# A recurrent attention and SiLU kernel: its 1449 steps in a written order with fixed PSUM tiles in place of a list scheduler

## The chip, the cores and the metric

The kernel runs on one core of a Trainium2 chip. The metric is device time of one execution in microseconds (us), measured several times; the profile comes from one more execution, recorded by the hardware profiler. Engines are named as in the profile: PE (TensorE matmuls), PEld (TensorE weight loads), DVE (VectorE), ACT (ScalarE), POOL (GpSimd), SP (SyncE, which here only issues transfers).

## The reference

Two blocks follow each other. The first is a recurrence over 768 tokens for 4 batches and 8 heads, with a state of 40 x 40 for each head; its output is the input of a dense block with a SiLU gate, 3072 tokens by 320 channels, 2048 hidden channels.

```
for t in range(S):
    y[:, :, t] = np.einsum('bhd,bhde->bhe', rt, state)
    Sa = np.einsum('bhde,bhe->bhd', state, at)
    state_decay = state * wt[:, :, None, :] - np.einsum('bhd,bhe->bhde', Sa, bt)
    state = state_decay + np.einsum('bhd,bhe->bhde', vt, kt)
x = y, as (4 * 768) rows of 8 * 40
h = x @ w_in
out = (h / (1 + exp(-h))) @ w_out
```

All inputs are float32 except `w_in` and `w_out`, which are float64.

## The kernel before

The sequence is cut into 12 chunks of 64 tokens. Within a chunk the recurrence is written as small matrix products, with a triangular system of 64 x 64 for each of 32 pairs of batch and head that has to be inverted. The code is a list of steps, each a Python function that issues a handful of instructions on one engine:

- `load(n)` and `load_r(n)` bring a chunk's inputs in (SP transfers of 512 KB, 96 KB and 160 KB).
- `prepare(n)` scales them on DVE (`down`, `between_` and `up` with the two scans of L627 and L645, the products of L654 and L664) and multiplies on PE (`between`, L682; `turn`, L769; `sv`, L744). The first product goes by way of DRAM (`ms<-sb`, L699).
- `special(n)`, for chunks 0 to 2, inverts the triangular systems: `xs<-ms` (L871) brings 16 x 16 blocks, DVE inverts them in a chain of short products and sums (`dots`, L795 and L796), `zs` and `mi` (L881, L887) carry them back, and PE and DVE then take turns three times (`more`, L958 on PE, the addition L973 on DVE). Before that DVE masks the block matrix `sb` (L900).
- `inverse(k)` and `merge(n)` do the same from chunk 3 on, for two chunks at once: a longer chain of L795 and L796 on DVE, transfers `zd`, `ZQ`, `xd` and `X`, then `merge` on PE (L1039, copies on ACT and DVE, L1068).
- `chain(n)` carries the state (PE L1111, L1135, L1166, L1196, L1223), `read(n)` makes the output of the recurrence (PE L1269, L1308, L1323; DVE masks of L1281 and the product of L1334).
- `moe(n)` is the dense block for 256 tokens: `full` (L1405) and `rest` (L1418), the gate on ACT (L1428), then `second` (L1445) and a copy to `ot` (L1457). One `full` is 8 matmuls of 128 x 128 by 256 columns, one `second` 4 of 128 x 128 by 320. The profile counts each float32 matmul as two instructions, so there a `full` is x16 and a `second` x8; the rows of the instruction order below count it once.
- `weights(n)`, ten units of 1 MB, fetches float64 weights with POOL transfers (L479) and puts them together as float32: DVE L484, L486, L487 and L493 or L500, ACT L485, L488 and L502, and for the first three units sums on PE (`sum_`, L508) with a product on DVE (L520).

PSUM is cut into four tiles of two banks each, called `pair`; two more tiles, `lam`, lie in SBUF. A step that needs one of them holds a `Room`, and the room gets its tile from whoever orders the steps.

What sets the order: each step says what it reads and writes, so that `Plan.add` knows which steps have to come before it. `Plan.order` is a list scheduler: it keeps an estimated clock for each engine, transfers and instruction fetches among the estimates, and takes the step that could start first, with a priority by chunk. `Plan.best(10, 400)` calls it 410 times when the kernel is built, with other weights and other priorities, values each order with the estimates of `Plan.through` and keeps the best. The steps are then issued in that order. Each engine works off its own instructions strictly in the order in which they were issued; SP, ACT and POOL also issue transfers, each its own queue in order. So the order that the scheduler writes is what each engine and queue follows, and an instruction that waits holds all those behind it on its engine.

```
    with tc.manual_schedule():
        for op in plan.best(10, 400):
            op["do"]()
```

Of the kernel before, what the change touches and what calls it, by code (L numbers as in the profile page):

```python
# [33 lines left out]
class Plan:  # L34
# [4 lines left out]
    def __init__(self, slots):  # L39
        self.slots = slots  # L40
        self.free = {k: [(0.0, i) for i in range(len(v))] for k, v in slots.items()}
        self.ops, self.wrote, self.read = [], {}, {}
# [23 lines left out]
    HOP = {"SP": 0.1, "ACT": 0.15, "PE": 0.15, "DVE": 0.15, "POOL": 0.2}  # L66
    RATE, LAND = 300.0, 2.0
    COLD = 42.0
    URGE = {"SP": 0.0, "ACT": 0.03, "PE": 0.05, "DVE": 0.1, "POOL": 0.02}
    LEAVE = {"F": 0.09, "R": 0.2, "T": 0.13, "Q": 0.13, "H": 0.12, "S": 0.11}  # L70
    ENTER = {"F": 0.08, "R": 0.1, "T": 0.03, "Q": 0.03, "H": 0.03, "S": 0.03}

    def turn(self, op):

        a, b = self.shape, op["shape"]
        if a == b or {a, b} == {"R", "T"}:
            return 0.03 if a != "F" else 0.0
        return self.LEAVE[a] + self.ENTER[b]

    def walk(self, start, cost, k, keep=False):  # L80


        fetched, count, t = self.fetched[-2:], self.count, start
        step, end = cost / max(k, 1) * (2 if start < self.COLD else 1), count + k
        have = len(self.fetched)
        while count < end:
            block = count // 256
            gate = 256 * block + 194
            if have == block + 1:
                fetched.append(max(t + 0.4, fetched[-1] + 2.6) + 1.3)  # L90
                have += 1
            if count >= gate:
                t = max(t, fetched[-1] + 0.1)
            to = min(end, gate if count < gate else 256 * block + 256)
            t += (to - count) * step
            count = to
        if keep:
            self.fetched += fetched[2:]
            self.count = end
        return t  # L100

    def order(self):
        ops = self.ops
        self.fetched, self.count, self.shape = [0.0, 0.0], 0, "Q"
        nexts = [[] for _ in ops]
        for op in ops:
            op["wait"] = len(op["before"])
            for b in op["before"]:
                nexts[b].append(op)
        ready = {e: [op for op in ops if op["engine"] == e and not op["wait"]] for e in self.HOP}  # L110
        at = dict.fromkeys(self.HOP, 0.0)
        out, held = [], {}
        queue = dict.fromkeys(("SP", "ACT", "POOL"), 0.0)
        for op in ops:
            op["ready"] = 0.0
        while len(out) < len(ops):
            best = None
            for e, some in ready.items():
                starts = []
                for op in some:  # L120
                    s = max(at[e], op["ready"])
                    for room in op["rooms"]:
                        if room.slot is None:
                            free = self.free[room.kind]
                            fits = free and held.get((room.kind, room.most), 0) < room.most
                            s = max(s, min(free)[0]) if fits else 1e9
                    lost = 0.0
                    if e == "PE" and s < 1e8:
                        lost = self.walk(s + self.turn(op), op["cost"], op["k"]) - s - op["cost"]
                    starts.append((s, s + lost, op))  # L130
                if not starts:
                    continue
                urge = self.URGE[e]
                s, _, op = min(starts, key=lambda x: (x[1] + urge * x[2]["pri"], x[2]["n"]))
                if best is None or s < best[0]:
                    best = s, op
            s, op = best
            assert s < 1e8, "no room"
            e = op["engine"]
            ready[e].remove(op)  # L140
            if e == "PE":
                at[e] = end = self.walk(s + self.turn(op), op["cost"], op["k"], True)
                self.shape = op["shape"]
            else:
                at[e] = end = s + op["cost"]
            if op["size"]:
                begin, work = max(queue[e], end), op["size"] / self.RATE
                both = max(0.0, max(queue[o] for o in queue if o != e) - begin)
                queue[e] = begin + (2 * work if work < both / 2 else work + both / 2)
                for o in queue:  # L150
                    if o != e and queue[o] > begin:
                        queue[o] += min(work, both / 2)
                end = queue[e] + self.LAND
            op["start"], op["end"] = s, end
            for room in op["rooms"]:
                if room.slot is None:
                    room.slot = self.free[room.kind].pop(self.free[room.kind].index(min(self.free[room.kind])))[1]
                    room.end = 0.0
                    held[room.kind, room.most] = held.get((room.kind, room.most), 0) + 1
                room.left -= 1  # L160
                room.end = max(room.end, end)
                if not room.left:
                    held[room.kind, room.most] -= 1
                    self.free[room.kind].append((room.end + 0.1, room.slot))
            for x in nexts[op["n"]]:
                x["ready"] = max(x["ready"], end + (self.HOP[x["engine"]] if x["engine"] != e else 0.0))
                x["wait"] -= 1
                if not x["wait"]:
                    ready[x["engine"]].append(x)
            out.append(op)  # L170
        return out

    SLOW = 2.8, 1.7
    CASES = (1.0, 300.0, 0.15, 1.0), (1.5, 240.0, 0.15, 1.0), (1.5, 240.0, 0.25, 1.04)
    WINDOW, FEW = 3.41, 0.42

    def through(self, out, crowd, rate, hop, slower):

        at = dict.fromkeys(self.HOP, 0.0)
        queue = dict.fromkeys(("SP", "ACT", "POOL"), 0.0)
        end, free = [0.0] * len(out), {}
        fetched, count, shape, work = [0.0, 0.0], 0, "Q", {}
        before, after = self.SLOW
        width, few = self.WINDOW, self.FEW
        for op in out:
            e = op["engine"]
            s = at[e]
            for b in op["before"]:  # L190
                s = max(s, end[b] + (hop if self.ops[b]["engine"] != e else 0.0))
            for place in op["takes"]:
# [39 lines left out]
    def best(self, draws, steps):  # L232

        rng = Random(1)
# [1425 lines left out]
```

## Time and profile before

| | us |
|---|---|
| median of 3 runs | 733.7 |
| lowest and highest | 732.0, 738.74 |
| span of the profiled execution | 734.2 |
| PE busy | 676.8 |
| PE idle before its first matmul | 13.7 |
| PE idle from 21 us on, up to 36.2 | 15.1 |
| last matmul ends, span ends | 726.2, 734.2 |
| DVE busy | 419.7 |
| ACT busy | 194.1 |

The page gives busy time for each engine, the granted TensorE clock in slices (PEclk), the load of the 16 DMA engines, the chain of work that ended last, and groups of equal instructions. Finer views of the same execution list instructions in order of time, with the idle time before them and what ended it, or give the busy time of every engine in chosen stretches. In such rows the first number is the start, the second the length, and "x64" the number of instructions. "issue" as the releaser means that the engine waited for nothing that the profile shows.

### The profile page before, as it was taken

The numbers are of one execution on the slowest core, as the hardware profiler recorded it, in microseconds if no ns is written. First come the engines' busy times: TensorE is split into PE (matmuls) and PEld (weight loads), VectorE is DVE, ScalarE is ACT, GpSimd is POOL, SyncE is SP. The second block draws the span as 40 slices with busy tenths as digits, with TensorE's granted clock in tenths as the row PEclk, the third lists the DMA queues.
The fourth block names the chain that finished last, engine by engine and source line by source line (L and its number), as shares of the span: only waits on it lengthen the run. The fifth ranks groups of instructions, "written<-read, shape, count | busy, mean of one in ns | idle before, by whom it ended". The sixth has DMA issues, their size and how long they took to land.

```text
span 734.2 us, 27298 instructions
## 1 busy us (share of the span) xinstructions
PE 676.8 (92%) x12666; PEld 542.3 (74%) x12666; DVE 419.7 (57%) x614; ACT 194.1 (26%) x241; POOL 15.2 (2%) x35
## 2 busy tenths in 40 slices
PE   2179899998999999999999999999999999999995
PEld 2177568787778678878778878778777778787773
DVE  6845799977469348397364883372992676020000
ACT  3251625422302413304312305132104312102020
POOL 2101000000000000000000000000000000000000
PEclk9996999999899999999999999999997999999998
DMA  7680754751721554417355306354215033201001
GB/s 249 150 235 27 205 194 128 223 128 37 177 93 25 137 138 141 126 46 162 81 136 142 103 19 145 87 149 130 66 27 119 26 103 108 44 20 41 18 1 22
DMA packets 117921, 77.15 MB, mean 105 GB/s; under 512 B 65538, under 2 KB 114229, under 8 KB 117160
## 3 DMA queue, kind: packets, MB, share of 16 engines
q1 hardware_dynamic: 113220, 64.43, 33.5%
q0 software_dynamic: 2224, 10.63, 4.4%
q8 instruction: 101, 1.65, 0.9%
q10 hardware_dynamic: 2356, 0.26, 0.3%
q14 instruction: 20, 0.16, 0.1%
HBM read 60.29 MB, written 14.61 MB: 102 GB/s over the span
## 4 chain that ended last, share of the span: by engine, by line
PE 86%; DVE 5%; ACT 3%; issue 2%; DMA 1%; SPq 1%; ACTq 0%; DVEq 0%
PE pair L1445 30%; PE pair L1405 23%; PE pair L1418 6%; PE pair L1269 4%; PE pair L682 3%; PE pair L1323 3%; PE pair L958 2%; PE pair L1223 2%; PE pair L744 2%; PE pair L1135 2%; PE pair L1068 2%; PE pair L1308 1%; PE pair L1111 1%; PE pair L1166 1%; PE pair L508 1%
## 5 line engine op out<-in xcount | busy, mean ns | idle before, releaser
L1445 PE MATMUL pair<-wo,gts 128*128 128x320 f32 x768 | 221.6, 445 | 0.2 <-issue 0.2
L1445 PEld LDWEIGHTS pair<-wo,gts 128*128 128x128 f32 x768 | 145.7, 193 | 60.5 <-issue 4.3
L1405 PE MATMUL pair<-xt,wi 128*128 128x256 f32 x768 | 176.6, 387 | 0.2 <-DVE wi L520 0.2
L1405 PEld LDWEIGHTS pair<-xt,wi 128*128 128x128 f32 x768 | 145.6, 192 | 22.8 <-issue 1.3
L1428 ACT ACTIVATE gts<-pair 128x1024 f32<-128x1024 f32 x48 | 46.5, 1020 | 107.5 <-PE pair L1418 100.4
L1457 DVE COPY ot<-pair 128x320 f32<-128x320 f32 x24 | 11.8, 491 | 95.2 <-PE pair L1445 93.5
L682 PE MATMUL pair<-a,kb 40*64 40x64 f32 x1536 | 33.5, 241 | 33.5 <-DVE a L654 28.7
L796 DVE TENSOR_REDUCE XI<-XI 128x64 f32<-128x512 f32 (+9 forms) x85 | 58.7, 690 | 2.9
L682 PEld LDWEIGHTS pair<-a,kb 40*64 40x64 f32 x1536 | 29.7, 153 | 36.6 <-issue 18.4
L1418 PE MATMUL pair<-xt,wi 64*128 64x256 f32 x384 | 47.9, 389 | 0.0
L1418 PEld LDWEIGHTS pair<-xt,wi 64*128 64x128 f32 x384 | 35.1, 187 | 6.3 <-issue 2.0
L1334 DVE TENSOR_TENSOR lam<-pair,wz 128x1024 f32<-128x1024 f32 x11 | 13.5, 1224 | 41.6 <-PE pair L1323 41.4
L1281 DVE TENSOR_TENSOR lam<-pair,ml 128x1024 f32<-128x1024 f32 x22 | 26.5, 1220 | 14.0 <-PE pair L1269 12.4
L795 DVE TENSOR_TENSOR XI<-XI,mi 128x1024 f32<-128x1024 f32 (+8 forms) x60 | 33.7, 561 | 1.5
L1269 PEld LDWEIGHTS pair<-r,vut 40*64 40x64 f32 x1536 | 26.3, 142 | 6.4 <-issue 4.8
L1269 PE MATMUL pair<-r,vut 40*64 40x64 f32 x1536 | 29.3, 228 | 1.1 <-issue 1.1
L664 DVE TENSOR_TENSOR kb<-kbv 128x512 f32<-128x512 f32 (+1 forms) x36 | 29.8, 860 | 0.2
L1001 ACT COPY mi<-XI 128x1024 f32<-128x1024 f32 x5 | 10.1, 2023 | 70.6 <-DVE XI L796 70.6
L627 DVE TENSOR_TENSOR_SCAN kbv<-wz,zt 128x1024 f32<-128x1024 f32 x12 | 27.5, 2292 | 0.5
L645 DVE TENSOR_TENSOR_SCAN wz<-wz,zt 128x1024 f32<-128x1024 f32 x12 | 27.5, 2291 | 0.4
L795 DVE TENSOR_TENSOR XI<-XI,xs 128x1024 f32<-128x1024 f32 (+1 forms) x25 | 25.2, 1009 | 0.7
L407 ACT ACTIVATE vu<-pair 64x640 f32<-64x640 f32 x13 | 9.1, 700 | 58.8 <-PE pair L1135 56.0
(152 smaller groups left out, 686.8 us busy)
## 6 DMA issues: line engine op xcount, KB each, us to landing
wz<-in_wT SPq DMA_DIRECT2D x12, 512.0 KB
kbv<-in_bT SPq DMA_DIRECT2D x12, 512.0 KB
a<-in_aT SPq DMA_DIRECT2D x12, 512.0 KB
kbv<-in_kT SPq DMA_DIRECT2D x12, 512.0 KB
r<-in_rT SPq DMA_DIRECT2D x48, 96.0 KB
vut<-in_vT SPq DMA_DIRECT2D x48, 96.0 KB
vu<-in_v SPq DMA_DIRECT2D x24, 160.0 KB
out<-ot SPq DMA_DIRECT2D x48, 80.0 KB
```

Of the source, the lines that this page charges most:

```text
L627: nc.vector.tensor_tensor_scan(back(V), back(W[:, 2 : 2 + Q * C]), zt, 1.0, ALU.mult, ALU.add)
L645: nc.vector.tensor_tensor_scan(Z, Z, zt, 0.0, ALU.mult, ALU.add)
L664: TTn[engine].tensor_tensor(out=at_(kb, place(is_b, first), (576 * step, 4 // step), (128, 4), (1, C)), in0=blocks((kf, bf)[is_b]), in1=bl ...
L682: nc.tensor.matmul(room.tile[half(b), j, g * C : g * C + C], lhsT=kb[rows(j), place(is_b, q) : place(is_b, q) + C], rhs=A[rows(j), q * C : ...
L795: nc.vector.tensor_tensor(out=at_(tmp, 0, *dims), in0=x, in1=y, op=ALU.mult)
L796: nc.vector.tensor_reduce(out=out_, in_=at_(tmp, 0, *dims), axis=AX.X, op=ALU.add)
L1269: nc.tensor.matmul(pl.tile[half(1 - b if role else b), b, c * C : c * C + C], lhsT=vut[rows(b), role, hu, :], rhs=rs[rows(b), hh, :], star ...
L1281: lambda pl=pl, la=la: nc.vector.tensor_tensor(out=la.tile.rearrange("p (q t) -> p q t", q=Q), in0=pl.tile.rearrange("p a b -> p (a b)").r ...
L1405: nc.tensor.matmul(rooms[g].tile[:, f // 2, (f % 2) * T : (f % 2) * T + T], lhsT=wi[:, k, (4 * g + f) * 128 : (4 * g + f) * 128 + 128], rh ...
L1418: nc.tensor.matmul(rooms[g].tile[:, h, (f % 2) * T : (f % 2) * T + T], lhsT=wi3[half(h), g * 256 + (f % 2) * 128 : g * 256 + (f % 2) * 128 ...
L1428: nc.scalar.activation(out=gts[:, 4 * g * T : 4 * g * T + 4 * T], in_=rooms[g].tile.rearrange("p a b -> p (a b)"), func=AF.Silu)
L1445: nc.tensor.matmul(po[b].tile[:, 0, 0:DM], lhsT=g4[:, f, 128 * b : 128 * b + 128], rhs=wo[:, f, :], start=f == 0, stop=f == NF - 1,)
```

## The change

The scheduler, its estimates and its search are taken out. In their place stands `Plan.follow`, which takes two tables written into the file: `ORDER`, the numbers of all 1449 steps in the order in which they are issued, and `SLOTS`, one digit for each room, the tile that it gets. The steps themselves, what each reads and writes, and every instruction and transfer that a step issues are the same as before: 383 steps on PE, 391 on DVE, 223 on ACT, 21 on POOL and 431 on SP. Only their order within each engine and queue changes, and which of the four `pair` tiles (or two `lam` tiles) a step uses. Lines after L262 move up by 144 (L958 becomes L814).

```diff
-    def order(self):
...
-    def through(self, out, crowd, rate, hop, slower):
...
-    def best(self, draws, steps):
...
+    def follow(self, order, slots):
+
         rooms = {id(room): room for op in self.ops for room in op["rooms"]}
+        assert sorted(order) == list(range(len(self.ops))) and len(slots) == len(rooms)
+        for room, slot in zip(rooms.values(), slots):
+            room.slot, room.tile = int(slot), self.slots[room.kind][int(slot)]
+        done = set()
+        for n in order:
+            assert self.ops[n]["before"] <= done
+            done.add(n)
+        return [self.ops[n] for n in order]
+
+ORDER = """
+0 3 2 1 84 86 5 7 6 8 116 12 9 10 11 13 15 14 117 90 31 16 29 22 20 23 17 91 25 24 19 21 18 92 118 30 94 33 85
...
+SLOTS = """
+03002133122302302010321213033023202300211303211223101103300221000023321202000110213203100101302001012022313320
...
     with tc.manual_schedule():
-        for op in plan.best(10, 400):
+        for op in plan.follow([int(n) for n in ORDER.split()], "".join(SLOTS.split())):
             op["do"]()
```

In the rows below the tile names carry the numbers of their buffers (`sb_90` is the block matrix of chunk 1, `sb_89` that of chunks 0 and 2; `pair_111` to `pair_114` are the four PSUM tiles).

The first place is the stretch in which chunk 0's inverse ends and chunk 1's begins, about 35 to 56 us, on SP and on DVE. SP before, the last of eight loads of `r` and `vut` and what follows them:

```order
L592 DMA r<-in_rT 48x2x256
L601 DMA vut<-in_vT 48x2x256
L575 DMA vu_100<-in_v 64x2x320 x2
L699 DMA ms<-sb_90 16x16x16 x8
L871 DMA xs<-ms 128x256
```

SP now, from the transfers `mi` of chunk 0's inverse on:

```order
L743 DMA mi<-zs 16x16x16 x4
L457 DMA vut<-in_vT 48x2x256
L555 DMA ms<-sb_90 16x16x16 x8
L727 DMA xs<-ms 128x256
L457 DMA vut<-in_vT 48x2x256
L448 DMA r<-in_rT 48x2x256
```

The eight pieces of `ms` and the `xs` behind them now come ahead of all but one of the loads of `r`, `vut` and `vu_100`. On POOL, which issued three 1 MB fetches of weights in a row here (one into `raw`, two into `wo`), the second fetch into `wo` now stands behind a transfer of `read(0)`'s result. DVE before, at the additions of `special(0)`, from the third to what follows the last:

```order
L973 TENSOR_TENSOR XI<-pair_112,X_94 128x4x128
L973 TENSOR_TENSOR XI<-pair_113,X_94 128x4x128
L973 TENSOR_TENSOR X_94<-pair_114,X_94 128x4x128
L973 TENSOR_TENSOR X_94<-pair_111,X_94 128x4x128
L900 TENSOR_TENSOR sb_90<-sb_90,ml 128x1024
L729 TENSOR_TENSOR lam_116<-pair_113,ml 128x1024
```

DVE now, from the first of these additions to the fifth:

```order
L829 TENSOR_TENSOR XI<-pair_113,X_94 128x4x128
L343 TENSOR_SCALAR gts<-gts 128x1024
L340 TENSOR_SCALAR wi<-wo 128x2x512
L829 TENSOR_TENSOR XI<-pair_114,X_94 128x4x128
L756 TENSOR_TENSOR sb_90<-sb_90,ml 128x1024
L829 TENSOR_TENSOR XI<-pair_111,X_94 128x4x128
L829 TENSOR_TENSOR XI<-pair_113,X_94 128x4x128
L340 TENSOR_SCALAR wi<-raw_137 128x2x512
L829 TENSOR_TENSOR X_94<-pair_114,X_94 128x4x128
```

Between the additions (L829) there now stand steps of the weights and the mask of `sb_90`, which came later before. A little earlier on DVE, `down`, `between_` and `up` of chunk 1 and its product into `a_84` now stand ahead of the chain of short products and sums of `special(0)`; before, `between_`, `up` and that product stood behind it.

The second place is PE at the third inverse, `special(2)`. Before, from its first product to the next `full`:

```order
L682 MATMUL pair_111<-a_83,kb 64x64 x32
L958 MATMUL pair_113<-XI 64x64 x32
L744 MATMUL pair_114<-vu_100,lam_115 64x40 x32
L958 MATMUL pair_111<-XI 64x64 x32
L769 MATMUL pair_113<-ident,kb 128x40 x16
L1405 MATMUL pair_114<-xt,wi 128x256 x8
```

Now:

```order
L1261 MATMUL pair_114<-xt,wi 128x256 x8
L538 MATMUL pair_111<-a_84,kb 64x64 x32
L814 MATMUL pair_112<-XI 64x64 x32
L1261 MATMUL pair_113<-xt,wi 128x256 x8
L814 MATMUL pair_111<-XI 64x64 x32
L1274 MATMUL pair_114<-xt,wi_67 128x256 x4
```

Long matmuls of `moe(1)` (L1261, L1274) now stand between the products of `special(2)`.

The third is PE at `merge(9)`. Before:

```order
L1405 MATMUL pair_112<-xt,wi 128x256 x8
L682 MATMUL pair_111<-a_85,kb 64x64 x32
L769 MATMUL pair_113<-ident,kb 128x40 x16
L1039 MATMUL pair_111<-ZQ,sb_90 32x32 x32
L769 MATMUL pair_113<-ident,kb 128x40 x16
L682 MATMUL pair_111<-a_85,kb 64x64 x32
L1068 MATMUL pair_113<-X_95,ZQ 32x32 x32
L1405 MATMUL pair_111<-xt,wi 128x256 x8
```

Now:

```order
L895 MATMUL pair_113<-ZQ,sb_90 32x32 x32
L1274 MATMUL pair_112<-xt,wi_67 128x256 x4
L1274 MATMUL pair_114<-xt,wi_67 128x256 x4
L1052 MATMUL pair_111<-ident,G 104x40 x16
L538 MATMUL pair_113<-a_85,kb 64x64 x32
L600 MATMUL pair_112<-vu_99,lam_116 64x40 x32
L924 MATMUL pair_114<-X_95,ZQ 32x32 x32
L1261 MATMUL pair_113<-xt,wi 128x256 x8
```

The two matmul steps of `merge(9)` (L1039 and L1068 before, L895 and L924 now) have other work between them than before, and on DVE the whole of `inverse(3)`, which ends ahead of them, now stands in front of the preparation of chunk 11 and no longer behind it.

More of the change, by code (lines that the diff above doesn't have):

```diff
@@ L3 @@
 from math import prod
-from random import Random
 import concourse.bass as bass
@@ L40, in __init__ @@
         self.slots = slots
-        self.free = {k: [(0.0, i) for i in range(len(v))] for k, v in slots.items()}
         self.ops, self.wrote, self.read = [], {}, {}
@@ L64, in add @@
         return op
[L66 to L100, printed above, removed]
@@ L102, in order @@
-    def order(self):
[L103 to L171, printed above, removed]
@@ L173 @@
-    SLOW = 2.8, 1.7
-    CASES = (1.0, 300.0, 0.15, 1.0), (1.5, 240.0, 0.15, 1.0), (1.5, 240.0, 0.25, 1.04)
-    WINDOW, FEW = 3.41, 0.42
-    def through(self, out, crowd, rate, hop, slower):
[L181 to L192, printed above, removed]
-                s = max(s, free.get(place, 0.0))
-            if e == "PE":
-                self.shape = shape
-                t, shape = s + self.turn(op), op["shape"]
-                to_ = count + op["k"]
-                step = op["cost"] / op["k"]
-                while count < to_:
-                    block = count // 256
-                    gate = 256 * block + 194
-                    if len(fetched) == block + 1:
-                        full = crowd if max(queue.values()) > t + 1 else 0.0
-                        fetched.append(max(t + 0.4, fetched[-1] + before) + after + full)
-                    if count >= gate:
-                        t = max(t, fetched[-1] + 0.1)
-                    to = min(to_, gate if count < gate else 256 * block + 256)
-                    left, count = (to - count) * step, to
-                    while left > 1e-9:
-                        w = int(t / width)
-                        pace = 0.5 if t > 30 and work.get(w - 1, 0.0) < few * width else 1.0
-                        d = min((w + 1) * width - t + 1e-9, left / pace)
-                        work[w] = work.get(w, 0.0) + d
-                        t += d
-                        left -= d * pace
-            else:
-                t = s + op["cost"] * (slower if e == "DVE" else 1.0)
-            at[e] = t
-            if op["size"]:
-                begin, work_ = max(queue[e], t), op["size"] / rate
-                both = max(0.0, max(queue[o] for o in queue if o != e) - begin)
-                queue[e] = begin + (2 * work_ if work_ < both / 2 else work_ + both / 2)
-                for o in queue:
-                    if o != e and queue[o] > begin:
-                        queue[o] += min(work_, both / 2)
-                t = queue[e] + self.LAND
-            end[op["n"]] = t
-            for place in op["gives"]:
-                free[place] = max(free.get(place, 0.0), t + 0.1)
-        return max(end)
```

55 lines of the change are left out of this document (4 added, 51 removed), and 56 rows, old and new, of the table ORDER.

## The prediction

> **What bounds the kernel now.** I read the page first, then the stretches of busy time, then the rows of PE in order of time, with what ended each idle time.
>
> ```profile
> PE 676.8 (92%) x12666; PEld 542.3 (74%) x12666; DVE 419.7 (57%) x614; ACT 194.1 (26%) x241; POOL 15.2 (2%) x35
> PE 86%; DVE 5%; ACT 3%; issue 2%; DMA 1%; SPq 1%; ACTq 0%; DVEq 0%
> 100.00:150.00 50.00, 47.28 (x843) 37.35 (x838) 45.86 (x65) 24.23 (x27) 1.59 (x3) 0.97 0.67 210
> 650.00:700.00 50.00, 50.00 (x527) 39.70 (x526) 5.06 (x6) 5.96 (x8) 0.00 (x0) 1.00 0.10 27
> ```
>
> PE is 86% of the chain that ended last, and from 650 to 700 us it is busy without a gap. The change removes no matmul, so it can only give back time in which PE stands still or runs slowly. PE stands still for 734.2 - 676.8 = 57.4 us. Of these the next rows fix the parts that an order can hardly touch:
>
> ```profile
> 13.66 3.69 PE L682 MATMUL pair<-a,kb 40*64 40x64 f32 x128 [13.66 <-DVE a L654]
> 36.16 1.99 PE L682 MATMUL pair<-a,kb 40*64 40x64 f32 x64 [15.07 <-DVE a L654]
> 726.85 1.11 SPq L1460 DMA_DIRECT2D out<-ot  x2
> ```
>
> 13.7 us before the first product, 15.1 us while DVE inverts chunk 0's blocks, and 8.0 us from the last matmul's end at 726.2 on, 0.6 for the copy and 7.4 for the last transfer. That leaves 57.4 - 13.7 - 15.1 - 8.0 = 20.6 us of PE gaps, spread from 46 to 560 us. The second loss is slow running. In the stretches the last three numbers are the granted clock, the DMA share and GB/s:
>
> ```profile
> 42.00:46.00 4.00, 3.49 (x94) 3.25 (x91) 1.38 (x2) 4.00 (x6) 0.00 (x0) 1.00 1.04 319
> 46.00:50.00 4.00, 3.25 (x106) 3.21 (x109) 2.07 (x3) 0.50 (x1) 0.00 (x0) 1.00 1.06 283
> 58.00:62.00 4.00, 4.00 (x104) 2.74 (x106) 0.61 (x1) 0.07 (x1) 0.00 (x0) 0.50 0.02 4
> 66.00:70.00 4.00, 4.00 (x121) 3.07 (x118) 1.77 (x6) 1.03 (x2) 0.00 (x0) 0.89 0.02 4
> 196.00:200.00 4.00, 3.85 (x129) 3.16 (x122) 2.05 (x2) 0.00 (x0) 0.00 (x0) 0.57 0.57 115
> 248.00:252.00 4.00, 4.00 (x70) 2.51 (x68) 0.00 (x0) 0.79 (x2) 0.00 (x0) 0.60 0.68 149
> 560.00:564.00 4.00, 4.00 (x118) 3.73 (x111) 0.18 (x1) 1.60 (x2) 0.00 (x0) 0.50 0.56 92
> ```
>
> Four times the clock falls to half: from about 53 to 67 us, around 196 to 203, 247 to 252 and 557 to 568. Each time PE had just stood still.
>
> **The first patch, 36 to 100 us.** Two waits for nothing but the next instruction come just after 8 us in which the DMA engines were full (share 1.04 and 1.06):
>
> ```profile
> 46.75 3.31 PE L958 MATMUL pair<-XI 64*64 64x64 f32 x102 [1.26 <-issue]
> 53.32 0.34 PE L1166 MATMUL pair<-X,R 64*40 64x64 f32 x3 [2.76 <-issue]
> 59.27 3.69 PE L1269 MATMUL pair<-r,vut 40*64 40x64 f32 x128
> 289.81 2.09 PE L1269 MATMUL pair<-r,vut 40*64 40x64 f32 x128
> 35.86 1.42 POOL L479 DMA_DIRECT2D wo<-in_w_in  x2
> wo<-in_w_in POOLq DMA_DIRECT2D x2, 1024.0 KB, 13.2
> 41.48 11.30 SPq L699 DMA_DIRECT2D ms<-sb  x8
> 54.42 1.23 DVE L900 TENSOR_TENSOR sb<-sb,ml 128x1024 f32<-128x1024 f32 x1 [3.62 <-DMA ms<-sb]
> ```
>
> The waits are 4.0 us. Behind them the half clock costs, from 53.3 to about 67 us (0.89 in the window 66 to 70 is 0.9 us of it): 14 us of PE work at 3.69 against 2.09 us for the same 128 matmuls, 14 x (1 - 2.09 / 3.69) = 6.1 us. Together 10 us. The load is three fetches of 1 MB (two of them 13.2 us on the way), eight loads of `r` and `vut` and two of `vu`, and behind all these eight small pieces of `ms` that took 11.3 us to issue. The change takes one 1 MB fetch out of this stretch and puts `ms` ahead of seven of the eight loads. At 300 GB/s, near the rates of the two full stretches, 1 MB is 3.5 us less to carry before the next instructions come. I take 6 of the 10 us: the wait of 2.76 us goes below the point at which the clock falls, the other stays. Bounds: all 10 (the matmul work at 45 us finds free DMA engines), or nothing (the loads are only shifted by a few us).
>
> [...]
>
> On DVE `special(1)` moves forward, and weights are put together in gaps in which DVE waited for PE:
>
> ```profile
> 43.72 0.69 DVE L973 TENSOR_TENSOR XI<-pair,X 128x512 f32<-128x512 f32 x1 [4.01 <-PE pair L958]
> 92.38 1.22 DVE L973 TENSOR_TENSOR XI<-pair,X 128x1024 f32<-128x1024 f32 x1
> 90.22 2.08 PE L958 MATMUL pair<-X,XI 64*64 64x64 f32 x64 [1.25 <-ACT X L405]
> 109.94 1.10 PE L1166 MATMUL pair<-X,R 64*40 64x64 f32 x64 [1.62 <-ACT gts L1428]
> ```
>
> The row at 92.38 is `special(1)`'s first addition. Its blocks come by way of `ms`, whose pieces ended 54 us in, so it can start earlier by what `ms` gains; from 100 to 150 us DVE is busy 45.86 of 50, so work done in the gaps before helps there. Of the PE gaps from 74 to 110 us (these two and five shorter ones, some 5 us) I take 3. Chunk 1's preparation also loses the scan of 2.3 us and more from the way between `special(0)`'s chain and its first product at 36.16, but gets two masks of 1.23 us and a weights step in return, and the first product of all comes a product later: 1 us, no more. Start in all: -10 us, bounds 0 and -18. What hides the moved weights steps is DVE's wait of 4.01 us; if the 1 MB for `wo` lands later than the additions need, DVE stands at that step (`wi<-wo`) and holds them up (first rival).
>
> **The second patch, 160 to 204 us.** Before, 992 matmuls in small products run with hardly a long one between them, and PE waits for instructions again:
>
> ```profile
> 167.99 0.63 PE L682 MATMUL pair<-a,kb 40*64 40x64 f32 x27 [0.86 <-issue]
> 171.81 0.61 PE L744 MATMUL pair<-vu,lam 64*64 64x40 f32 x28 [0.81 <-issue]
> 195.79 1.25 PE L682 MATMUL pair<-a,kb 40*64 40x64 f32 x60 [0.92 <-issue]
> 199.79 14.69 PE L1445 MATMUL pair<-wo,gts 128*128 128x320 f32 x47 [0.15 <-issue]
> 523.70 17.49 PE L1445 MATMUL pair<-wo,gts 128*128 128x320 f32 x64
> ```
>
> Gaps of 0.86 + 0.81 + 0.92 and 0.4 us for one more, 3.0 us. Then 47 matmuls take 14.69 us where 47 / 64 x 17.49 = 12.8 would do, 1.9 us more, and the small products ahead of them, at 0.57 in the window 196 to 200, some 1 us more: 3 us of half clock. Now `full`, `rest` and the first `second` of `moe(1)` stand between the products. I take 5 of the 6 us; bounds 0 and 6.
>
> **The merges at 246 and 557 us.** The four small steps around `merge(9)` wait for each other:
>
> ```profile
> 547.97 1.22 DVE L796 TENSOR_REDUCE XI<-XI 128x128 f32<-128x1024 f32 x1
> 246.31 0.69 PE L769 MATMUL pair<-ident,kb 40*128 40x40 f32 x16 [0.81 <-DVE ZQ L409]
> 557.15 0.75 PE L1039 MATMUL pair<-ZQ,sb 32*32 32x32 f32 x64 [0.72 <-DVE lam L729]
> 559.34 1.99 PE L682 MATMUL pair<-a,kb 40*64 40x64 f32 x64 [0.81 <-DVE ZQ L409]
> 563.10 6.44 PE L1405 MATMUL pair<-xt,wi 128*128 128x256 f32 x16
> 550.99 3.72 PE L1405 MATMUL pair<-xt,wi 128*128 128x256 f32 x16
> ```
>
> 1.5 us of waits, then 6.44 - 3.72 = 2.7 us lost on one `full` and by the same ratio 1.6 on the two small steps before it: 5.8 us. Now `inverse(3)` stands ahead of chunk 11's preparation on DVE (two scans and four products, some 10 us), and the two halves of the merge have `rest`, L1052, L538 and L600 between them. The merge near 246 has a wait of 0.8 us and a patch of 4 us at 0.60, which is 3.2 us at half clock and 1.4 lost: 2.2 us. I take 7 of the 8.0; bounds 0 and 8.0.
>
> **What comes in.** The other waits of PE for instructions (six short ones, some 3 us in all) stay, since the small steps between long ones are as many as before:
>
> ```profile
> 353.10 0.62 PE L682 MATMUL pair<-a,kb 40*64 40x64 f32 x26 [0.83 <-issue]
> ```
>
> Two runs of small products grow to 672 matmuls, at chunks 5 and 7; a run of about that length cost this 0.83 us and no patch. The tables were fixed for one set of moments and the chip has its own: I add 3 us, bounds 0 and 7 (one more patch like that at 557, 5.8).
>
> **Sum.** -10 - 5 - 7 + 3 = -19: the profiled 734.2 goes to 715. The median 733.7 lies 0.5 under the profiled span, so the forecast for the runs is 715. Ends: 733.7 - (18 + 6 + 8) = 702, 733.7 + 7 = 741. A measurement of this kernel tells about 1% from no change, 7.3 us: faster means under 726.4, slower over 741.
>
> **Rivals.** First, the start gains nothing. If the first fetch into `wo` again takes 13.2 us from 35.2, it lands at 48.4; three additions, the mask and a second weights step then follow, some 6 us, and `special(0)` ends at 55 where it ended at 50.8. That eats the 6 us of the clock patch, and the three us on DVE stay in doubt: start 0, sum 733.7 - 9 = 725, with 720 to 735 around it. For it speaks that DVE works in order; against it that only 2 MB are under way, not 3.
>
> Second, the start gains more. If DVE runs without gaps from 50 us on, the additions of `special(1)` come some 10 us before 92.38, and `moe(1)`, which begins at 150.5, comes 15 to 17 us sooner. With the other terms (-5, -7, +3) that is a sum of -25 or so, 708, and down to 702 with less coming in. Against it speaks that PE and DVE take turns in it.
>
> ```profile
> 150.51 7.07 PE L1405 MATMUL pair<-xt,wi 128*128 128x256 f32 x32
> ```
>
> Third, slower: half clock patches where none is now. Each costs 4 to 10 us with its gap (the four above). The order is tight everywhere, and a transfer that comes 2 us late in a run of small products is enough, as at 53 us. To be slower than 741 the kernel must have about as much lost in patches as now, and two new ones of 5 us on top: from the sixth on. For it speaks that runs of 672 matmuls appear; against it that 300 to 550 us had only short waits and no patch at runs as long.
>
> That the change does nothing is excluded: the order differs on every engine.
>
> **Chances.** The forecast (710 to 724) 0.58, start gains nothing 0.19 (a third of it still under 726.4), start gains more 0.14, slower patches 0.09. Faster 0.58 + 0.14 + 0.06 = 0.78, same 0.13, slower 0.09. The range leaves out one in ten above and one below: 702 to 731.
>
> **What would show it.** In the profile after: no `issue` wait over 2 us and no clock under 0.9 between 50 and 66 us; the addition of `special(1)` before 86 us; the first `full` of `moe(1)` 8 to 12 us before 150; no patch at the place of `special(2)` or of `merge(9)`. A DVE wait over 3 us at the weights step between the additions of `special(0)` would show the first rival, five or more clock patches the third.

## The result, and the profile after

| | before | after |
|---|---|---|
| median, us | 733.25 (4 runs, 732.0 to 738.74) | 703.77 (4 runs, 702.16 to 707.02) |
| span of the profiled execution, us | 734.2 | 700.4 |
| PE busy, us | 676.8 | 654.6 |

The ratio of the runs is 0.9569, with a 95% interval of 0.9511 to 0.9626: 29.5 us, where the forecast had 19. The profiled executions differ by 33.8 us.

From the profile's page, the busy time of each engine and the engines' shares of the chain that ended last:

```profile
PE 654.6 (93%) x12666; PEld 532.4 (76%) x12666; DVE 417.6 (60%) x614; ACT 193.9 (28%) x241; POOL 18.1 (3%) x35
PE 88%; DMA 5%; DVE 2%; SPq 1%; issue 1%; ACT 1%; POOL 0%; DVEq 0%; POOLq 0%
q8 instruction: 101, 1.65, 1.0%
```

The same 12,666 matmuls keep PE busy for 22.2 us less, so most of the gain isn't idle time but cheaper work. The third line is the queue that carries instructions; it will matter below. The stretches (start and end, length, then PE, weight loads, DVE, ACT and POOL busy, the granted clock, DMA share, GB/s):

```profile
36.00:60.00 24.00, 18.77 (x428) 15.39 (x422) 13.90 (x31) 10.79 (x15) 1.91 (x3) 0.93 0.50 142
60.00:100.00 40.00, 35.81 (x838) 27.16 (x832) 33.21 (x36) 17.29 (x21) 5.48 (x8) 0.96 0.65 178
150.00:200.00 50.00, 49.94 (x1200) 41.77 (x1199) 38.70 (x59) 16.31 (x22) 1.12 (x2) 1.00 0.38 102
200.00:250.00 50.00, 50.00 (x981) 40.77 (x982) 30.88 (x38) 14.00 (x18) 0.00 (x0) 1.00 0.45 119
500.00:550.00 50.00, 50.00 (x979) 41.33 (x978) 28.31 (x47) 13.88 (x17) 0.00 (x0) 1.00 0.45 115
```

From 110 us to the last matmul the clock never falls, and PE has one wait of 0.47 us. The rows that answer to those of the prediction (start, length, and in brackets the wait before and its releaser):

```profile
45.77 0.69 DVE L340 TENSOR_SCALAR wi<-wo 128x1024 int32<-128x1024 int32 x1
50.31 1.23 DVE L756 TENSOR_TENSOR sb<-sb,ml 128x1024 f32<-128x1024 f32 x1 [3.25 <-DMA ms<-sb]
52.19 3.39 PE L814 MATMUL pair<-XI 64*64 64x64 f32 x64 [3.06 <-DVE XI L829]
83.27 1.23 DVE L829 TENSOR_TENSOR XI<-pair,X 128x1024 f32<-128x1024 f32 x1 [0.51 <-PE pair L814]
87.04 3.27 PE L1261 MATMUL pair<-xt,wi 128*128 128x256 f32 x7 [3.35 <-DMA vut<-in_vT]
106.08 3.72 PE L1261 MATMUL pair<-xt,wi 128*128 128x256 f32 x16 [1.18 <-ACT gts L1284]
142.18 3.62 PE L1261 MATMUL pair<-xt,wi 128*128 128x256 f32 x16
521.25 0.75 PE L895 MATMUL pair<-ZQ,sb 32*32 32x32 f32 x64
521.93 2.00 PE L1274 MATMUL pair<-xt,wi 64*128 64x256 f32 x16
526.26 1.20 PE L924 MATMUL pair<-X,ZQ 32*32 32x32 f32 x64
```

`special(1)`'s first addition comes at 83.27 (92.38 before), `moe(1)` begins at 142.18 (150.51 before), and `merge(9)` runs without a wait. The start has three new waits of its own: 3.25 us of DVE for `ms`, 3.06 and 3.35 us of PE.

**Where the 33.8 us lie.** To compare stretches in which the steps stand in another order, I gave each kind of matmul a price: what it takes from its start to the next one's where PE doesn't wait, from 150 us on (the 30% quantile over the profiles; about 15 ns in L538, 222 in L1261, 275 in L1301). Time that has passed, less the prices of all matmuls started, is what was lost until then:

| stretch, us | lost before | lost after | difference |
|---|---|---|---|
| 0 to 140 | 58.2 | 52.2 | -6.0 |
| 140 to 200 | 7.4 | 1.5 | -5.9 |
| 200 to 240 | 2.1 | 0.2 | -1.9 |
| 240 to 260 | 4.0 | 0.1 | -3.9 |
| 260 to 540 | 10.6 | 3.0 | -7.6 |
| 540 to 580 | 7.0 | 0.3 | -6.7 |
| 580 to the tail | 1.9 | 0.1 | -1.8 |

From 140 us on the old order lost 10.5 us in waits (5.9 with "issue" as the releaser, 4.0 on DVE, 0.7 on ACT), 7.8 at half clock, and 14.8 in matmuls that took longer than their price at full clock. After, these are 0.5, 0 and 4.5. What slows the matmuls of the last group was not tried by itself.

### The profile page after: what moved, and what is told of

It reads as the page before. It is cut to its first block, busy times and chain, and to the rows that moved or that the text cites. A ratio compares the mean times of both kernels' runs of the same rounds, so it can differ in the third digit from the quotient of the medians.

```text
span 700.4 us, 27219 instructions
## 1 busy us (share of the span) xinstructions
PE 654.6 (93%) x12666; PEld 532.4 (76%) x12666; DVE 417.6 (60%) x614; ACT 193.9 (28%) x241; POOL 18.1 (3%) x35
## 3 DMA queue, kind: packets, MB, share of 16 engines
q8 instruction: 101, 1.65, 1.0%
## 4 chain that ended last, share of the span: by engine, by line
PE 88%; DMA 5%; DVE 2%; SPq 1%; issue 1%; ACT 1%; POOL 0%; DVEq 0%; POOLq 0%
PE pair L1301 30%; PE pair L1261 25%; PE pair L1274 7%; PE pair L538 4%; PE pair L1125 4%; PE pair L1179 3%; PE pair L1079 2%; PE pair L814 2%; PE pair L625 2%; PE pair L1022 2%; PE pair L1164 1%; PE pair L600 1%; PE pair L924 1%; PE pair L991 1%; PE pair L967 1%; DMA ms<-sb 1%
## 5 line engine op out<-in xcount | busy, mean ns | idle before, releaser
L1301 PE MATMUL pair<-wo,gts 128*128 128x320 f32 x768 | 216.7, 437 | 0.0
L1301 PEld LDWEIGHTS pair<-wo,gts 128*128 128x128 f32 x768 | 143.3, 190 | 57.2 <-issue 0.7
L1261 PE MATMUL pair<-xt,wi 128*128 128x256 f32 x768 | 176.1, 385 | 4.5 <-DMA vut<-in_vT 3.4
L1261 PEld LDWEIGHTS pair<-xt,wi 128*128 128x128 f32 x768 | 145.0, 191 | 26.9 <-issue 3.8
L1274 PE MATMUL pair<-xt,wi 64*128 64x256 f32 x384 | 47.9, 389 | 0.0
L538 PE MATMUL pair<-a,kb 40*64 40x64 f32 x1536 | 30.5, 232 | 15.1 <-ACT kbv L531 14.5
L538 PEld LDWEIGHTS pair<-a,kb 40*64 40x64 f32 x1536 | 27.1, 145 | 21.6 <-ACT kbv L531 14.5
L1274 PEld LDWEIGHTS pair<-xt,wi 64*128 64x128 f32 x384 | 35.2, 187 | 4.9 <-issue 0.7
L638 ACT COPY kt<-pair 128x640 f32<-128x640 f32 x24 | 16.6, 692 | 49.5 <-PE pair L625 49.5
L1125 PEld LDWEIGHTS pair<-r,vut 40*64 40x64 f32 x1536 | 24.2, 135 | 3.2 <-issue 2.2
L1125 PE MATMUL pair<-r,vut 40*64 40x64 f32 x1536 | 26.3, 220 | 0.0
L600 PE MATMUL pair<-vu,lam 64*64 64x40 f32 x768 | 14.6, 232 | 12.5 <-DVE lam L585 12.0
```

What stands on the lines that cost most here:

```text
L538: nc.tensor.matmul(room.tile[half(b), j, g * C : g * C + C], lhsT=kb[rows(j), place(is_b, q) : place(is_b, q) + C], rhs=A[rows(j), q * C : ...
L1125: nc.tensor.matmul(pl.tile[half(1 - b if role else b), b, c * C : c * C + C], lhsT=vut[rows(b), role, hu, :], rhs=rs[rows(b), hh, :], star ...
L1261: nc.tensor.matmul(rooms[g].tile[:, f // 2, (f % 2) * T : (f % 2) * T + T], lhsT=wi[:, k, (4 * g + f) * 128 : (4 * g + f) * 128 + 128], rh ...
L1274: nc.tensor.matmul(rooms[g].tile[:, h, (f % 2) * T : (f % 2) * T + T], lhsT=wi3[half(h), g * 256 + (f % 2) * 128 : g * 256 + (f % 2) * 128 ...
L1301: nc.tensor.matmul(po[b].tile[:, 0, 0:DM], lhsT=g4[:, f, 128 * b : 128 * b + 128], rhs=wo[:, f, :], start=f == 0, stop=f == NF - 1,)
```

## Experiments

The first nine keep every step as it is and change `ORDER` or `SLOTS` alone; the last six do one small step more than once, with the same result. Ratios are to the kernel before on the same chip; its medians there were 734.5 to 738.6 us, so ratios, not times, are compared with the 0.957 of the change. The cuts of code give each edit in short: `OLD` and `NEW` stand for the orders before and after, `OLD_SLOTS` for the tiles before, and the kernels hold the finished tables. Where two orders are joined or steps of the new one are moved on PE, 8 to 89 of the 312 tiles also differ from the change's (`slots`).

**Which part of the order?** The two orders joined at the first product of `moe(1)`, in two runs:

```diff
-for op in plan.follow(ORDER, SLOTS):
+for op in plan.follow(NEW[:375] + [n for n in OLD if n not in NEW[:375]], slots):
```

> The changed kernel's first 375 steps (up to the first product of the dense block for chunk 1, 142 us in its profile), then the 1074 others in the order in which the kernel before has them. Theory (the gain lies after 150 us, where waits of PE for instructions and half-clock patches are gone): the start alone brings what that first product came earlier, 8 us, so 733.3 - 8 = 725 us, with the half-clock patch and the waits near 165 to 200 us back. Rival (a better start lets everything behind it follow without waits): near the changed kernel, 700 to 708 us.

741.66 us (10 runs), ratio 1.008 (1.004 to 1.012): 0.8% slower than before, where the theory had 725 us. Part of it is a wait of 8.15 us where the changed kernel, with the same order up to there, had 3.35, so transfers at the start vary by some us from run to run. Behind the joint the old waits are back:

```profile
93.53 6.12 PE L1261 MATMUL pair<-xt,wi 128*128 128x256 f32 x16 [8.15 <-DMA xt<-X]
168.71 0.44 PE L538 MATMUL pair<-a,kb 40*64 40x64 f32 x11 [0.76 <-issue]
```

```diff
+for op in plan.follow(OLD[:395] + [n for n in NEW if n not in OLD[:395]], slots):
```

> The kernel before's first 395 steps (up to the same product, 150 us in its profile), then the others in the changed kernel's order. Theory: all of the steady part's gain without the start's, 733.3 - 22 = 711 us (708 to 714). Rival (the start carries the gain): 725 to 733 us. A third case, that the two halves fit badly where they are joined, would show as waits of PE at 140 to 170 us.

708.14 us, ratio 0.963 (0.955 to 0.970). The order behind `moe(1)`'s first product makes nearly all of the gain; the new start adds some 4 us by the medians, which is not clear of the noise, and nothing when the old order follows it.

```diff
+for op in plan.follow(NEW[:375] + sorted(NEW[375:690], key=OLD.index) + NEW[690:], slots):
```

> The changed kernel with one stretch in the kernel before's relative order: its steps 375 to 690, about 142 to 240 us, in which chunk 2's inverse is finished and ten small PE steps then stand in a row. Theory: that train of small steps brings back the PE waits of 0.4 to 0.9 us for instructions and the half-clock patch seen there before, some 5 us of waits and 2 us of clock, so 703.8 + 7 = 711 us. Rival (the order inside that stretch is no cause, the gain is spread over later stages): 702 to 706 us.

728.06 us, ratio 0.989 (0.982 to 0.997), much more than the theory's 711. The old waits are back up to 300 us, and where the stretch joins the new order PE waits 4.67 us more for a mask:

```profile
315.78 1.95 PE L1164 MATMUL pair<-r,GT 40*40 40x64 f32 x64 [4.67 <-DVE lam L1137]
```

By the table's prices this profile lost 26.8 us from 140 to 320 us (13.1 up to 240) and 3.5 from 320 to 680, where the changed kernel lost 3.3. So a stretch's loss is made in the stretch.

```diff
+for op in plan.follow(NEW[:1110] + sorted(NEW[1110:1410], key=OLD.index) + NEW[1410:], slots):
```

> The changed kernel with its steps 1110 to 1410 (from 480 us of its profile to nearly the end) in the relative order of the kernel before, on all engines. Theory (the order inside each stretch makes its loss): the waits at the merge of chunk 9 and the half-clock patch of 10 us behind it come back, which in the kernel before cost some 8 us between 500 and 640 us, so 703.8 + 8 = 712 us. Rival (the stretch inherits its ease from the lead that the inverses have by then): 702 to 706 us.

722.29 us, ratio 0.983 (0.976 to 0.989): 19 us worse than the change, where 8 were expected. All of PE's waits of over 0.2 us behind 240 us lie in that stretch, and each is for DVE; three of the seven:

```profile
489.94 1.10 PE L1164 MATMUL pair<-r,GT 40*40 40x64 f32 x64 [1.90 <-DVE lam L1137]
509.66 10.77 PE L1301 MATMUL pair<-wo,gts 128*128 128x320 f32 x39 [1.14 <-DVE R L977]
545.29 1.74 PE L538 MATMUL pair<-a,kb 40*64 40x64 f32 x64 [0.81 <-DVE ZQ L265]
```

**The tiles.**

```diff
-SLOTS = """
-03002133122302302010321213033023202300211303211223101103300221000023321202000110213203100101302001012022313320
+SLOTS = (the tile that has been free longest; 148 of 312 differ)
```

> The changed kernel's order with other tiles: each step that needs a PSUM or lam tile gets the one that has been free longest, which changes the tile of 148 of 312. Theory: the written tiles are no cause of the gain, within 1% of 703.8 us. Rival (which tile a step gets decides what it waits for): over 708 us, with PE waits on DVE and ACT after 110 us, where the changed kernel has none.

706.83 us, ratio 0.962 (0.955 to 0.969). From 120 us on PE waits 1.45 us, 0.64 of it ahead of its last two instructions. Its profile has 8.42 us at the start for `xt<-X`. The gain doesn't hang on the written tiles.

**Mending the start.** Four steps moved (190, 193 and 187 leave their later places), and in a second run two more:

```diff
-199 219 134 77
...
-200 201 75 114
+199 134 77
...
+200 201 75 219 114
...
-177 166 218
+177 190 193 187 166 218
```

> The changed kernel with four steps moved at the start: the DVE mask of chunk 1's block matrix behind the last addition of chunk 0's inverse, and the three ACT transfers of the recurrence's output for chunk 0 ahead of the conversions of weights on ACT. Theory: PE's waits of 3.06 us (at 52.19 us) and 3.35 us (at 87.04 us) go, with about 1.5 us of half clock behind the first, so 703.8 - 8 = 696 us. Rival (another input is late just behind each): PE waits for something else at the same two places and the time stays within 702 to 705 us.

702.46 us, ratio 0.956 (0.949 to 0.963): no gain on the change. Both waits are gone, and PE stands at other places instead:

```profile
95.12 3.63 PE L814 MATMUL pair<-XI 64*64 64x64 f32 x64 [2.79 <-DVE XI L829]
104.28 3.72 PE L1261 MATMUL pair<-xt,wi 128*128 128x256 f32 x16 [1.18 <-ACT gts L1284]
231.94 0.38 PE L1022 MATMUL pair<-X,R 64*40 64x64 f32 x10 [1.41 <-issue]
```

```diff
-239 311 240 271 313 227
+239 227 311 240 271 313
...
-372 333 242 274
+372 274 333 242
```

> The run e4_start_mended with two more moves: DVE's second addition of chunk 1's inverse ahead of the scaling that waits for a load of chunk 2, and ACT's first gate ahead of a copy. In that run PE had waited 2.79 us (at 95.12 us) for the addition and 1.18 us (at 104.28 us) for the gate. Theory (PE is the bound from 110 us on, so what the start gains stays): 702.5 - 3.5 = 699 us. Rival (something else is late just behind, or PE's packets come late later on): 701 to 704 us.

702.79 us, ratio 0.957 (0.954 to 0.961). The rival held again: the next waits are 1.17, 1.85 and 1.12 us from 96 to 103 us, two for ACT's copy of `kt`, one for an addition. At the start the chain through DVE, ACT and the loads is as long as PE's, whichever wait is taken out.

**Runs of small products.** I had seen that instructions come in packets (101 on queue q8), and that PE waits where small products run long (0.86, 0.81 and 0.92 us between 167 and 196 us in the kernel before). Two kernels moved only steps of the dense block on PE, ten in the old order to break such runs and fifteen in the new one to lengthen them. One place of each:

```diff
 890 chain6.turn
+811 moe5.full
 897 read6.look
 899 read6.write_state
-811 moe5.full
```

> The order of the kernel before, tiles too, written out, with ten steps of the dense block moved by one to four places on PE from chunk 1 on, and nothing else. They break up runs of small products. Theory (supply: PE's instructions come in packets of 16 KB, about 127.5 matmuls, of which the profiles show none closer than 3.3 us to the last, so a packet whose matmuls need less than about 3.5 us of PE makes PE wait): the ten moves cut the waits that this rule gives for the old order from 7.4 to 1.2 us, and a part of the half clock behind them, so 6 to 9 us faster: 734 - 7 = 727 us. Rival (DVE's and the transfers' order bring the gain, runs of small products are harmless): 732 to 736 us.

744.0 us, ratio 1.013 (1.008 to 1.019): 1.3% slower, against the theory. Long waits for instructions stay (1.99 and 1.96 us), and the waits for DVE from 140 us on grow from 4.0 to some 12 us: a long step that leaves its place uncovers the step that it had hidden.

```profile
164.98 1.02 PE L538 MATMUL pair<-a,kb 40*64 40x64 f32 x27 [1.99 <-issue]
345.35 1.63 PE L1022 MATMUL pair<-X,R 64*40 64x64 f32 x64 [1.66 <-DVE X L265]
```

```diff
 703 moe4.second
 709 moe4.second
+710 moe4.second
 704 moe4.second
 863 prepare7.between
 953 prepare8.between
 883 chain6.right
-710 moe4.second
```

> The opposite: the changed kernel with 15 steps of the dense block moved by one to four places on PE from 211 us on, so that small products stand in longer runs; the other engines' and queues' orders stay. Theory (supply): the rule of 3.5 us for 127.5 matmuls gives 15 us of PE waits in about 17 places, with 'issue' as the releaser and of 0.2 to 1.7 us each; with some half clock behind them 703.8 + 15 = 719 us (714 to 724). Rival (runs of small products are harmless): 702 to 706 us, and no new waits with 'issue'.

736.59 us (10 runs), ratio 1.001 (0.997 to 1.005): fifteen steps moved by at most four places take back the whole gain, twice what was expected. Waits with "issue" are some 5 us, those for DVE, ACT and transfers more than twice that. So this pair doesn't separate the two causes: PE's order was moved, and with it what every other engine was waited for.

**The borders of the instruction packets alone.** In the profiles before and after queue q8 carries 101 packets, 1.65 MB or 16 KB each, one for some 125 of the 12,666 matmuls. PE's waits with "issue" stand on a grid of nearly the same step: in the kernel before, from 150 us on, they end at matmul 2762, 2889, 3529, 3657, 4803, 6334, 6462, 7354, 9395 and 9778 (counted from 0), and every difference from one to the next is within 3 of a multiple of 127.45. I take this grid for the borders of the packets. The two waits in the first patch (46 and 53 us) end at 474 and 602, 128 apart. No two packets start closer than 3.3 us (at the least 3.32 us in the profile before, 3.40 after). In the profiles before, after, and of the runs with 32 and 64 extra matmuls below, each of the 45 waits of over 0.15 us with "issue" behind 140 us ends 1.2 to 1.6 us after a packet was carried. From this an estimate, called the rule from here on: PE gets past a border no sooner than 3.5 us after it starts the matmul 24 places ahead of the border before. Both figures are chosen to suit the waits of the kernel before, and no run measures either by itself (with 3.5 us and 32 matmuls the rule has 1.1, 0.9, 0.8 and 0.5 us at matmuls 6337, 6465, 7357 and 9396, the trace 0.83, 0.63, 0.86 and 0.43 within 3 of them); 16 to 32 matmuls give the ranges below.

The rule says that the new order has no such wait at all as its borders lie, and 5 to 14 us with the matmuls 16 to 96 places further on; the old order has 6 to 10 us wherever the borders lie. That can be tried without moving a step: one step done more than once, up to 25 us, while PE would wait until 32 us anyway. Nothing that waits for anything moves.

```diff
         for op in plan.follow([int(n) for n in ORDER.split()], "".join(SLOTS.split())):
             op["do"]()
+            for _ in range(1 if op is plan.ops[25] else 0):
+                op["do"]()
```

> The changed kernel with one step done twice: the second `between` product of chunk 0, 64 matmuls, again into the same tile, at about 20 us, where PE then waits until 32 us. The output is the reference's. No order changes; only every later matmul moves on by 64 places against the borders of the instruction packets (about 127.5 matmuls each). Theory (the written order fits the borders: each packet holds 3.5 us of PE work or more only where the borders lie now): the rule of 3.5 us gives 10 to 14 us of new PE waits with 'issue' after 210 us, with half clock behind some, so 703.8 + 13 = 717 us (712 to 724). Rival (the order keeps PE fed whatever the borders): 702 to 706 us, since the 1 us of extra work lies in an idle stretch.

732.46 us (10 runs), ratio 0.995 (0.991 to 0.999): 1 us of extra work in an idle stretch takes back 26 to 29 us of the 29.5, twice what was expected. From 107 us on every wait of PE in its profile is for instructions, and some end at the counts of the old order: 2765, 3531 and 4807 here, 2762, 3529 and 4803 there. One place, first in the changed kernel, then in this one:

```profile
242.53 6.73 PE L1301 MATMUL pair<-wo,gts 128*128 128x320 f32 x24
249.19 2.10 PE L538 MATMUL pair<-a,kb 40*64 40x64 f32 x128
251.21 0.75 PE L895 MATMUL pair<-ZQ,sb 32*32 32x32 f32 x64
251.89 2.42 PE L1301 MATMUL pair<-wo,gts 128*128 128x320 f32 x8
```

```profile
249.83 5.82 PE L1301 MATMUL pair<-wo,gts 128*128 128x320 f32 x21
255.58 2.09 PE L538 MATMUL pair<-a,kb 40*64 40x64 f32 x128
257.60 0.74 PE L895 MATMUL pair<-ZQ,sb 32*32 32x32 f32 x63
259.73 0.18 PE L895 MATMUL pair<-ZQ,sb 32*32 32x32 f32 x1 [1.39 <-issue]
259.85 2.42 PE L1301 MATMUL pair<-wo,gts 128*128 128x320 f32 x8
```

The instructions are the same. The wait here ends at matmul 4807; twice 127.45 ahead of that, at 4552, the changed kernel has a border between the 24 long matmuls and the 128 small ones. A packet starts at 245.86, while the long ones still run, and the next at 252.29, when all the small ones are done. With 64 more, the borders fall into the small ones: a packet starts at 257.55, is carried by 258.51, and PE goes on at 259.73, one matmul short of the long ones.

Two controls, the step done three times, and the same edit in the old order:

```diff
+            for _ in range(2 if op is plan.ops[25] else 0):
```

> The same step done three times, 128 extra matmuls, so that the borders fall half a matmul from where they fell. Theory: the rule gives no new waits, 702 to 706 us, though twice the extra work of the run with 64. Rival (the extra work itself, or its place at the start, costs): slower than the run with 64 extra matmuls.

708.35 us, ratio 0.965 (0.961 to 0.969), 2 us above the theory's range and far below the rival's. Twice the extra work costs about a fifth as much, queue q8 carries one packet more (102), and waits for instructions after 200 us are 0.8 us. In its profile 5.0 of the 6 us against the changed kernel are lost by 140 us, with two new waits, 2.26 and 0.93 us, at matmuls 352 and 416.

```diff
-for op in plan.follow(NEW, SLOTS):
+for op in plan.follow(OLD, OLD_SLOTS):
```

> The kernel before's order and tiles, written out, with the same step done twice, 64 extra matmuls. Theory: the old order doesn't fit the borders anywhere: the rule of 3.5 us gives 5 to 7 us of waits after 150 us with the borders here as there, so 734 us, within 1% (727 to 741). Rival (the extra matmuls disturb any order's start): slower by about what the same edit costs the changed kernel.

736.93 us (10 runs), ratio 1.001 (0.998 to 1.005). The shift costs the old order nothing.

Then the size of the cost against the shift, with another small step (16 matmuls) repeated:

```diff
+            for _ in range(1 * (op is plan.ops[29])):
```

> The changed kernel with one `turn` step of chunk 0 (16 matmuls) done twice, before PE's long wait at the start; the output is the reference's. Theory (fit to the borders): the rule of 3.5 us gives 5 to 6 us of new PE waits with 'issue' after 200 us, in 5 to 7 places; the run with 64 extra matmuls paid 26 us for 18 us of waits, so 8 us here: 712 us (708 to 717). Rival (any shift off the borders costs the same): 728 to 733 us. Second rival (no effect of the borders): 702 to 706 us.

```diff
+            for _ in range(2 * (op is plan.ops[29])):
```

> The same `turn` step done three times, 32 extra matmuls. Theory: 9 to 11 us of waits in 9 to 12 places, with the same ratio 15 us: 719 us (714 to 725), between the runs with 16 and with 64. Rival (any shift costs the same): 728 to 733 us.

```diff
+            for _ in range(3 * (op is plan.ops[29]) + 1 * (op is plan.ops[25])):
```

> The `turn` step done four times and the second `between` product of chunk 0 twice, 112 extra matmuls, more than in the run with 64, and 15 short of a whole packet. Theory: 0 to 4 us of waits: 703 to 710 us. Rival (any shift off the borders costs the same): 728 to 733 us. Second rival (the cost grows with the extra work at the start): over 732 us.

| extra matmuls | waits by the rule, us | "issue" waits after 200 us | median, us | ratio (95%) |
|---|---|---|---|---|
| 0 (the change) | 0 | 0.5 in 1 place | 703.8 | 0.957 (0.951 to 0.963) |
| 16 | 5 to 6 | 5.0 in 5 | 712.4 | 0.966 (0.960 to 0.973) |
| 32 | 9 to 11 | 12.8 in 12 | 724.8 | 0.985 (0.978 to 0.992) |
| 64 | 10 to 14 | 14.7 in 18 | 732.5 | 0.995 (0.991 to 0.999) |
| 112 | 0 to 4 | 1.0 in 2 | 705.6 | 0.959 (0.952 to 0.966) |
| 128 | 0 | 0.8 in 1 | 708.4 | 0.965 (0.961 to 0.969) |

The cost follows the rule shift by shift, up and down again; with 32 and 64 the waits are a little longer than the rule has them. The rule isn't exact: at matmul 4166, at 231.94 us, the run with the start mended waited 1.41 us, where the changed kernel, with the same order on PE, had no wait. Some of the waits in the run with 32:

```profile
267.06 0.33 PE L967 MATMUL pair<-G,a 40*64 40x40 f32 x2 [2.73 <-issue]
335.89 0.39 PE L895 MATMUL pair<-ZQ,sb 32*32 32x32 f32 x23 [1.22 <-issue]
560.33 0.54 PE L1164 MATMUL pair<-r,GT 40*40 40x64 f32 x21 [1.30 <-issue]
```

By the table the time lost is 1.6 to 2.0 times these waits with 16, 32 and 64. In the profile with 64 the waits from 140 us on are 15.9 us and the matmuls beside them take 10.2 us over their price where the changed kernel's take 4.5; that one took 725.84 us. Seven of its nine other executions show a granted clock of 0.979 to 0.987 against 0.990, so half clock behind the waits is likely to make up the rest; there is no profile of those.

## Why the prediction was right and where it was wrong

Direction and the place of the bound were right: PE gave back waits, half clock and slow matmuls. The steps:

- **Start, -10.** Measured -6.0 up to 140 us: the term was too large. The waits for instructions of 1.26 and 2.76 us went (the longest is now 1.47), the first addition of `special(1)` came before 86 us and `moe(1)` 8.3 us sooner, as forecast. But half clock stayed, for 3.4 us from 52.6 on and for 3.4 us from 86.7 on. That it would go with a shorter wait was an estimate from two waits (1.26 us at 46.75, with full clock behind it up to 50 us, and 2.76 us at 53.32, with half clock); how long PE waits doesn't decide it alone, since in the kernel before half clock also followed a wait of 0.72 us, at 557.15. Moving `ms` ahead of the loads brought its pieces in at 49.9 us, and DVE's mask, which now stood between two additions, waited 3.25 us for them: the first rival's mechanism, at the mask and not at the weights step. The earlier `moe(1)` was no lead either: the two joined orders show that the start alone is worth nothing with the old order behind it and some 4 us with the new. Nor did the time come by the second rival, though 703.8 lies where that one had it (708, down to 702): it needed a start that gains more and `moe(1)` 15 to 17 us sooner. The prediction's four half-clock patches were five; it left out 3.4 us from 131.7 on.
- **Second patch, -5.** Measured -5.9 from 140 to 200 us; no patch, as forecast.
- **Merges, -7.** The stretches around them (240 to 260, 540 to 580) gave 10.6. Mechanism as forecast: long steps between the halves. The size was too small, since only the visible waits and one slowed `full` were priced.
- **What comes in, +3.** This step failed. It said that PE's other waits for instructions stay, "since the small steps between long ones are as many as before". The remaining stretches (200 to 240, 260 to 540, 580 on) gave 11.3 us instead of costing 3, and these 14 us are nearly all of what lies between the forecast sum of -19 and the 33.8 of the profiles. Visible waits there fell from 3.5 to 0.5 us; the rest is half clock and matmuls over their price, and how much of that the borders make stays open. The number of small steps doesn't decide; what does is where the borders fall among them and what runs just ahead: the same steps in the same order had 0.5 us of "issue" waits after 200 us, and 14.7 us with the borders moved by 64 matmuls. The two runs that the prediction has grow to 672 matmuls are 336 each in the profile (its number is twice that, as its 992 is twice the 496 from 160 us on). At 333 and 437 us they cost the changed kernel nothing, and 1.3 and 1.1 us with 64 extra matmuls ahead. In the kernel before, the positions listed above would have shown the period of 127.45 matmuls, and with it that an order can be free of these waits.
- In the same step the tables were said to be tight, so that new lateness would come in. They are tight (fifteen small moves cost 33 us), but no new lateness came in: from 110 us on the changed kernel has one wait, of 0.47 us, and it is for instructions.

The end of the first of the two runs of 336, in the changed kernel and then with 64 extra matmuls:

```profile
338.78 1.16 PE L538 MATMUL pair<-a,kb 40*64 40x64 f32 x64
```

```profile
348.68 0.58 PE L538 MATMUL pair<-a,kb 40*64 40x64 f32 x24
350.21 0.81 PE L538 MATMUL pair<-a,kb 40*64 40x64 f32 x40 [0.95 <-issue]
```

The first part also laid the waits at 46 and 53 us to full DMA engines (from 42 to 50 us; the first wait lies inside that stretch, not behind it). Load may add to them there: the packet ahead of the wait of 2.76 us started at 50.87 us, 4.1 us after the border at 46.75, where it was 1.2 us at 167.99. That was not tried by itself. After 140 us full engines aren't needed for a wait as long: the run with 32 has one of 2.73 us at 267 us behind 5 us with a DMA share of 0.67, and the shifts changed no transfer's order.

Two things make the gain, then. The new order leaves no wait for DVE or ACT behind 110 us; but with its borders moved by 64 it pays 15 us for instructions instead, and the sum is the old time. Where it fits the borders it pays neither. With the borders about where, by the rule, they suit it worst, what is left of the gain is some 4 us (ratio 0.995). How the written order came to fit them is not on record.

## What to carry to other kernels

Where PE works off many small products, count its instructions: if "issue" waits stand a fixed number of them apart (here within 3 matmuls of multiples of 127.45) and end just behind a packet (here 1.2 to 1.6 us), the supply is the likely bound. Here 192 small products behind 24 long matmuls cost no wait with borders 0 and 128 places into them, and 1.39 us with borders 64 and 191 places into them. An order that fits the borders can lose its gain by where it stands: 64 matmuls more ahead of this one, 1 us of work, took back 26 to 29 of its 29.5 us. So after each edit measure again, and try a shift by some idle repeats before an edit is judged. Price a stretch by what its matmuls take from start to start, not by its visible waits alone: from 140 us on the old order lost 10.5 us in waits and 22.6 us at half clock and in slow matmuls.

## What the runs showed of the hardware

- The supply of instructions to PE: packets of 16 KB (101 in 1.65 MB), none closer than 3.3 us to the last, against 2.0 us that 128 of the small products in L538 took (from 249.19 to 251.21 in the changed kernel). After one border at which PE had to wait, the next packet started 1.2 us later (matmul at 167.99, packet at 169.15), took 1.3 us (0.9 to 1.5 for the packets of the other such waits in that profile), and PE went on 1.4 us after it (packet carried by 170.45, matmul at 171.81).
- Half clock came in lengths near multiples of 3.4 us: up to the last matmul the clock records of these profiles show 3.4, 6.8, 10.2 and 13.7 us. In the kernel before, those of 13.7 us (from 53.2) and 10.2 us (from 558.4) are four and three times 3.4, with PE recorded as busy for 13.56 and 9.43 us of them; what sets the length was not tried.
- The start isn't the same from run to run: with one order up to there, PE's wait at about 87 to 93 us, ahead of a product with `xt`, was 3.35, 2.95, 2.49, 2.88 and 8.15 us in five profiles.
